# One task list with early positions of its own, and weight tiles loaded one by one into the freed tiles of high and low halves

## Chip, cores and metric

The kernel runs on one core of one Trainium2 chip. The metric is the device time of one execution in microseconds (us); the median of the runs is quoted, and a profile of one execution stands behind all rows.

## What is computed

Attention over 8 batches of 8 heads (576 positions, head size 64) with rotary embedding, followed by a soft mixture of experts over all 4608 tokens:

```python
q_rot, k_rot = rotate(q), rotate(k)
attn = softmax(q_rot @ k_rot.T / sqrt(64)); x = (attn @ v) as [4608, 512]
logits = x @ phi                              # 8 experts x 4 slots
slot_input = softmax(logits, tokens).T @ x
slot_out[e] = relu(slot_input[e] @ w1[e]) @ w2[e]     # w1: 8x512x1024, w2: 8x1024x512
out = softmax(logits, slots) @ slot_out
```

## The kernel before

The 64 heads are worked as 32 **pairs**. For each pair p the kernel runs the same set of named tasks:

- `load0`, `load1` (line 144, SyncE's queue SP): q and k of the pair into the tile `x_in`, of which there are two; so the load of pair p+2 waits until pair p has left `x_in`.
- `spin0`, `spin1` (L149, GpSimd, here POOL): products with cosine and sine, four instructions each; `join` (L153, VectorE, here DVE): their sum.
- `high0`, `high1` (L158, ScalarE, here ACT): casts of q and k to 16 bits, written into a tile `hl`; `low` (L162, DVE): what the casts lost, into the same `hl`, after which `x_in` is free.
- nine m units (`m00` to `m31`, `m_rem`): four matmuls on TensorE (PE, L182 or L190) of high halves into one of three score tiles `s_ps` in PSUM, and a DVE reduction (L184 or L192) that reads it; then `m_min` (DVE, L196), `m_turn` (PE, L203), `m_half` (ACT, L207) and `m_rows` (two DMAs on SP, L212 and L213), which put the row maxima into the tile `peak`.
- nine t units (`t0` to `t8`): sixteen matmuls (L229), the last four with `peak`, into an `s_ps`, and an exponential on ACT (L230) into `a_t`.
- nine `av` units (L245, PE): times v into `o_ps`; then `o_out` (ACT, L253), sums (`add1`, `add2` on DVE, `total` on PE, L273, `total_out` on ACT, L278), and the division by way of DRAM (`send`, `spread`, `widen` on SP, `norm` on POOL).

The engines take their instructions in the order in which the program issues them. That order comes from the table `WHEN`: a position for every task, in beats of which one pair has four. In the main loop `beat` sorts the tasks by their position within a beat, and pair p's round issues each task for the pair that is due. Ahead of the loop stands code written out by hand: 23 dummy matmuls on PE (`heat(N_WARM)`, L634), the m units of pair 0 mixed with parts of pair 1, then 16 dummy matmuls (`heat(16)`), then `join`, `high0` and four m units of pair 1, and then all tasks whose position is negative.

The mixture needs 64 weight tiles of 512 KB. `load_w` loads them in the order of the list `order`: 24 during the pairs, 7 into the space that `x_in` leaves (`release_io`, by `trickle`). When the last pair is through with its t units, `release_stk` gives up the pool of the four `hl` tiles and loads four more there: one tile `wk`, then three. `release_att` then loads the constant `seg` and nine tiles (pool `wl`); the rest follow as the first 24 tiles are used. Behind the pairs, PE works through `ffn1` (L782), `ffn2_steps` (L806) and `combine` (L834), which runs twice over nine blocks of the output: the first time mixed with `ffn2_steps`, the second time after the last of them. Each combine block is copied to SBUF and sent out by a DMA of 512 KB.

Of the kernel before, what the change touches and what calls it, by code (L numbers as in the profile page):

```python
# [29 lines left out]
N_XT = 3  # L30
N_WA = 5
N_WB = 2
N_WE = 3
N_WL = 9
N_X = 4
N_CS = 1
# [31 lines left out]
def attn_softmoe(ctx, tc, qk, v, phi, w1, w2, cs, ident, sel, seg, out):  # L68
# [10 lines left out]
    trans = ctx.enter_context(ExitStack())  # L79
    vp = trans.enter_context(tc.tile_pool(name="vp", bufs=2))  # L80
    att = trans.enter_context(tc.tile_pool(name="att", bufs=1))
    early = ctx.enter_context(ExitStack())
    stk = early.enter_context(tc.tile_pool(name="stk", bufs=4))
    right = ctx.enter_context(ExitStack())
    io = right.enter_context(tc.tile_pool(name="io", bufs=1, side="right"))
    dram = ctx.enter_context(tc.tile_pool(name="dram", bufs=3, space=bass.MemoryType.DRAM))
# [392 lines left out]
    order[N_W:N_W] = swap[:-1]
    order.insert(N_W + N_CST + N_WA, swap[-1])  # L480

    def load_w(pool, bufs, tag="w_exp"):
        n = order[len(w_tiles)]
# [12 lines left out]

    def release_io():
        right.close()
        wa = ctx.enter_context(tc.tile_pool(name="wa", bufs=N_CST, side="right", reuse_waits="tile"))
        wx = ctx.enter_context(tc.tile_pool(name="wx", bufs=N_WA, side="right", reuse_waits="tile"))  # L500
        extra.extend((wx, wa))
        later.extend([(wa, N_CST)] * N_CST + [(wx, N_WA)] * N_WA)

    def trickle(p):
        if later:
            load_w(*later.pop(0))

    def release_stk():
        early.close()
        hx = ctx.enter_context(tc.tile_pool(name="hx", bufs=1, side="right", reuse_waits="tile"))  # L510
        extra.append(hx)
        load_w(hx, 1, "wk")
        we = ctx.enter_context(tc.tile_pool(name="we", bufs=N_WE, side="right", reuse_waits="tile"))
        for _ in range(N_WE):
            load_w(we, N_WE)

    def release_att():
        trans.close()
# [37 lines left out]
    def one(task):  # L556
# [56 lines left out]
    beat = sorted((when % 4, int(when // 4), name) for name, when in WHEN.items())  # L613

    load(0)
    for t, cc in ((1, 0), (1, 1), (0, 0), (0, 1)):
# [15 lines left out]
    def heat(n):  # L632
        for i in range(n):
            nc.tensor.matmul(o[:, 0, 0:HC], lhsT=lift, rhs=halves[0][:, KH, 0:HC], start=True, stop=True)  # L634

    heat(N_WARM)
    low(0)
    done.update((n, 0) for n in ("spin0", "spin1", "join", "high0", "high1", "low", "load0", "load1"))
    do("load0", 2)
    do("load1", 2)  # L640
    nc.sync.dma_start(out=phi_sb, in_=phi.rearrange("(c p) n -> p c n", p=P))
    nc.sync.dma_start(out=sel_sb, in_=sel)
    do("spin1", 1)
    do("spin0", 1)
    for j in range(4):
        for n in range(2):
            do(f"m{j}{n}", 0)
        if j == 2:
            join(1, 1)
            do("high1", 1)  # L650
    do("m_rem", 0)
    do("m_min", 0)
    do("m_turn", 0)
    do("m_half", 0)
    m_rows(0, nc.scalar)
    done.add(("m_rows", 0))
    heat(16)
    join(1, 0)
    done.add(("join", 1))
    do("high0", 1)  # L660
    for j in range(2):
        for n in range(2):
            do(f"m{j}{n}", 1)
    do("low", 1)
    do("load0", 3)
    do("load1", 3)
    do("spin0", 2)
    do("spin1", 2)
    for when, name in sorted((when, name) for name, when in WHEN.items()):
        for p in range(NPAIR):  # L670
            if when + 4 * p < 0:
                do(name, p)

    for p in range(NPAIR):
        for _, back, name in beat:
            do(name, p - back)
        if not extra and ("low", NPAIR - 1) in done:
            release_io()

    p = NPAIR - 1  # L680
# [1 line left out]
        trickle(p)  # L682
    while pending:
        step(p)
    release_stk()
    for name in ("add1", "add2", "av4", "av5", "av6", "total", "total_out", "av7", "av8", "o_out"):
        do(name, p)
    steady.close()
# [252 lines left out]
```

## Time and profile before

| | us |
|---|---|
| median of 3 runs (lowest, highest) | 581.12 (580.03, 581.63) |
| the profiled execution: its time | 580.32 |
| the profiled execution: its span | 578.5 |
| busy in the span: PE, DVE, ACT, POOL | 527.7, 426.9, 330.7, 286.6 |

The profiled execution takes 1.8 us more than its span, and is 0.8 us below the median. The stages follow each other in the span: about 12 us until the first m unit, then a start in which the pairs get into step, then 30 pairs in a steady rhythm, then from about 500 us the mixture. A row of a timeline gives start, duration, engine, line and instruction; "x6" merges six of a kind, and brackets hold the idle time before and who ended it. SPq rows are the issue of a DMA, not its transfer. A row of windows gives one stretch: length, busy time of each engine with its count, TensorE's granted clock (1.00 is 2.4 GHz, 0.50 is 1.2 GHz), the share of the DMA engines and GB/s.

### The profile page before, as it was taken

To read this page: it belongs to the slowest core of one execution; us is meant where nothing else is said; L and a number is where in the kernel's file an instruction comes from. 1 tells how busy PE (TensorE), PEld (TensorE's weight loads), DVE (VectorE), ACT (ScalarE), POOL (GpSimd) and SP (SyncE) were. 2 spreads that over 40 slices of the span, in tenths; PEclk is the share of its full clock that TensorE was granted. 3 is DMA by queue.
4 is the path that set the end of the run, shared out by engine and by line. 5 is a ranking of instruction groups with operands and counts; after the bars stand their busy time and mean duration, and the time that the engine had idled before them with its cause. 6 is when DMAs were issued, how large, how long until landed. Compare 5 with 4: busy or idle time off the path is not lost.

```text
span 578.5 us, 23626 instructions
## 1 busy us (share of the span) xinstructions
PE 527.7 (91%) x10310; PEld 353.2 (61%) x10310; DVE 426.9 (74%) x643; ACT 330.7 (57%) x640; POOL 286.6 (50%) x332
## 2 busy tenths in 40 slices
PE   4669999999999998999999999999999999889991
PEld 2347667667766676666676767676766665634551
DVE  5788788889887897888889988988888752342261
ACT  2146557566657665766566666666666666315651
POOL 2865575576666685655655766566657010011100
PEclk9679999999999999999999999999999999989996
DMA  7244555555555555655655556555634245699999
GB/s 253 85 164 128 184 183 184 184 184 184 184 183 183 184 185 180 187 183 147 202 177 170 186 178 202 171 175 184 191 127 130 66 137 156 206 350 349 349 366 301
DMA packets 71735, 111.65 MB, mean 193 GB/s; under 512 B 20176, under 2 KB 47568, under 8 KB 71632
## 3 DMA queue, kind: packets, MB, share of 16 engines
q1 hardware_dynamic: 71618, 110.15, 59.0%
q8 instruction: 81, 1.33, 0.9%
q14 instruction: 22, 0.18, 0.1%
q10 hardware_dynamic: 14, 0.00, 0.0%
HBM read 99.93 MB, written 9.58 MB: 189 GB/s over the span
## 4 chain that ended last, share of the span: by engine, by line
PE 63%; DVE 12%; DMA 11%; ACT 6%; SPq 3%; issue 3%; POOL 0%; DVEq 0%; ACTq 0%
PE o_ps L245 17%; PE s_ps L229 17%; PE s_ps L273 7%; PE s_ps L182 5%; DMA rc<-s 4%; DVE nm L184 4%; DMA x_in<-in_qk 3%; SPq L284 3%; DVE hl L162 3%; PE s_ps L347 2%; PE s_ps L782 2%; DMA r_row<-rr 2%; PE s_ps L365 2%; ACT xn L356 1%; DVE x_in L153 1%
## 5 line engine op out<-in xcount | busy, mean ns | idle before, releaser
L149 POOL TENSOR_TENSOR x_in<-x_in,cs_sb 128x288 f32<-128x288 f32 x248 | 214.9, 899 | 130.8 <-DMA x_in<-in_qk 115.9
L184 DVE TENSOR_REDUCE nm<-s_ps 128x2 f32<-128x576 f32 x256 | 182.7, 751 | 55.7 <-PE s_ps L182 55.5
L230 ACT ACTIVATE a_t<-s_ps 128x576 f32<-128x576 f32 x256 | 160.8, 651 | 84.5 <-PE s_ps L229 72.8
L229 PE MATMUL s_ps<-hl 64*64 64x288 f16 x3456 | 160.1, 286 | 7.3 <-ACT xn L356 5.0
L245 PE MATMUL o_ps<-a_t,v_in 64*64 64x288 f32 x2048 | 163.6, 407 | 0.7 <-ACT xt L253 0.3
L229 PEld LDWEIGHTS <-hl 64*64 64x64 f16 x3456 | 102.0, 107 | 43.5 <-issue 28.8
L182 PE MATMUL s_ps<-hl 64*64 64x288 f16 x1024 | 84.5, 295 | 13.0 <-DVE nm L184 9.0
L229 PE MATMUL s_ps<-peak,lift 64*64 64x288 f16 x1152 | 91.9, 284 | 1.5 <-DMA peak<-mr 1.4
L307 POOL TENSOR_TENSOR xt<-xt,rb 128x576 f32<-128x576 f32 x30 | 48.8, 1626 | 71.3 <-DMA rb<-r_row 61.7
L245 PEld LDWEIGHTS o_ps<-a_t,v_in 64*64 64x64 f32 x2048 | 72.9, 133 | 17.1 <-ACT xt L253 4.5
L182 PEld LDWEIGHTS <-hl 64*64 64x64 f16 x1024 | 45.5, 106 | 36.7 <-issue 20.3
L158 ACT CAST hl<-x_in 128x576 f16<-128x576 f32 (+1 forms) x66 | 43.1, 655 | 24.4 <-DVE x_in L153 22.6
L153 DVE TENSOR_TENSOR x_in<-x_in 128x1152 f32<-128x1152 f32 (+2 forms) x36 | 54.6, 1517 | 2.7 <-POOL x_in L149 2.2
L278 ACT ACTIVATE s<-s_ps,bits 128x576 f32<-128x576 f32 x32 | 23.7, 742 | 48.3 <-PE s_ps L273 24.2
L260 DVE TENSOR_TENSOR c_t<-a_t 128x1152 f32<-128x1152 f32 x32 | 46.5, 1454 | 0.0
L162 DVE TENSOR_TENSOR hl<-x_in,hl 128x1152 f16<-128x1152 f32 x32 | 44.7, 1398 | 1.8 <-ACT hl L158 1.8
L229 PEld LDWEIGHTS <-lift 64*64 64x64 f16 x1152 | 40.3, 107 | 4.0 <-issue 2.6
L273 PE MATMUL s_ps<-a_t,pick 128*32 128x288 f32 x384 | 36.7, 406 | 0.0
L253 ACT COPY xt<-o_ps 128x576 f32<-128x576 f32 x32 | 20.5, 640 | 13.7 <-PE o_ps L245 13.7
L192 DVE TENSOR_REDUCE nm<-s_ps 128x2 f32<-128x576 f32 x32 | 24.1, 753 | 2.1 <-PE s_ps L190 0.9
L273 PEld LDWEIGHTS s_ps<-a_t,pick 128*32 128x32 f32 x384 | 16.4, 110 | 14.3
L263 DVE TENSOR_TENSOR c_t<-c_t,a_t 128x576 f32<-128x576 f32 x32 | 24.0, 750 | 0.1
(174 smaller groups left out, 536.4 us busy)
## 6 DMA issues: line engine op xcount, KB each, us to landing
x_in<-in_qk SPq DMA_DIRECT2D x62, 576.0 KB
w_exp<-in_w SPq DMA_DIRECT2D x63, 512.0 KB
v_in<-in_v SPq DMA_DIRECT2D x32, 576.0 KB
rb<-r_row SPq DMA_DIRECT2D x60, 144.0 KB
out<-w_exp SPq DMA_DIRECT2D x16, 512.0 KB
rc<-s SPq DMA_DIRECT2D x120, 4.5 KB
x_in<-in_qk SPq DMA_DIRECT2D x4, 288.0 KB
out<-w_exp SPq DMA_DIRECT2D x4, 256.0 KB
```

The lines of the kernel that those rows point to most:

```text
L149: eng.tensor_tensor(out=x[:, :, c], in0=x[:, :, c], in1=cs_sb[:, :, c], op=ALU.mult)
L153: nc.vector.tensor_tensor(out=x[:, t, 0, c], in0=x[:, t, 0, c], in1=x[:, t, 1, c], op=ALU.add)
L158: nc.scalar.copy(out=halves[p][:, 1 + t, c], in_=loaded[p][:, t, 0, c])
L162: nc.vector.tensor_tensor(out=hl[:, 0:4:3], in0=x[:, :, 0], in1=hl[:, 1:3], op=ALU.subtract)
L182: nc.tensor.matmul(s[rows[c], h, 0:HC], lhsT=hl[rows[h], QH, at:at + D], rhs=hl[rows[h], KH, half[n]], start=True, stop=True)
L184: nc.vector.tensor_reduce(out=nms[p][:, n, j:8:4], in_=s[:, :, 0:HC], axis=AX.X, op=ALU.max, negate=True)
L229: nc.tensor.matmul(s[rows[h ^ n], n, 0:HC], lhsT=lhs, rhs=rhs, start=(i == 0), stop=(i == 3))
L230: nc.scalar.activation(out=weights_of(p, b).rearrange("p (n x) -> p n x", n=2), in_=s[:, :, 0:HC], func=AF.Exp, scale=SCALE)
L245: nc.tensor.matmul(o[rows[h], n, 0:HC], lhsT=vt[r, b, n], rhs=a[r, half[n]], start=(b == 0), stop=(b == KB - 1))
L260: nc.vector.tensor_tensor(out=cts[p], in0=ats[p, 0], in1=ats[p, 1], op=ALU.add)
L273: nc.tensor.matmul(s[32 * i:32 * i + 32, n, 0:HC], lhsT=pick[:, n:n + NS], rhs=parts[cut][:, half[n]], start=first, stop=last, tile_positi ...
L307: eng.tensor_tensor(out=xts[p], in0=xts[p], in1=rbs.pop(p), op=ALU.mult)
```

## The change

**One list.** A second table, `EARLY`, gives the tasks of the first four pairs positions of their own, the dummy matmuls and constants among them. All tasks are put into one list, sorted and issued; the code by hand and `beat` are gone. From about pair 3 on, the order on every engine is that of before.

**Weight tiles in freed `hl` tiles.** The pool `stk` of the `hl` tiles is never given up. A new task `reuse` at beat 4.1 of pairs 28, 29 and 30 loads one weight tile into the `hl` tile of that pair, and after the last pair a fourth follows. `wk` becomes an `hl` tile; the pools that lie behind it move, and the load of `seg` has no tile to wait for any more.

```diff
+EARLY = {
+    "consts": (-31.889,), "heat0": (-31.727,), "spin1": (None, -30.178, -8.102, -2.333),
+    "low": (-29.941, -14.757, 0.917, 3.519), "load0": (None, None, -29.48, -13.395),
...
+    stk = ctx.enter_context(tc.tile_pool(name="stk", bufs=N_STK))
...
-    early = ctx.enter_context(ExitStack())
-    stk = early.enter_context(tc.tile_pool(name="stk", bufs=4))
...
-    def release_stk():
-        early.close()
-        hx = ctx.enter_context(tc.tile_pool(name="hx", bufs=1, side="right", reuse_waits="tile"))
-        extra.append(hx)
-        load_w(hx, 1, "wk")
-        we = ctx.enter_context(tc.tile_pool(name="we", bufs=N_WE, side="right", reuse_waits="tile"))
-        for _ in range(N_WE):
-            load_w(we, N_WE)
+    def reuse_stk(p):
+        if p >= NPAIR - N_STK:
+            load_w(stk, N_STK, "hl", swap[-1] if p == NPAIR - N_STK else None)
...
+        "reuse": lambda p: p < NPAIR - 1 and reuse_stk(p),
...
-    heat(N_WARM)
-    low(0)
...
-    heat(16)
-    join(1, 0)
-    done.add(("join", 1))
-    do("high0", 1)
...
-    for p in range(NPAIR):
-        for _, back, name in beat:
-            do(name, p - back)
+    seq = [(at, name, p) for name, ats in EARLY.items() for p, at in enumerate(ats) if at is not None]
+    early_set = {(name, p) for _, name, p in seq}
+    seq.extend((when + 4 * p, name, p) for name, when in WHEN.items() for p in range(NPAIR)
+               if (name, p) not in early_set and when + 4 * p < 4 * NPAIR)
+    seq.sort()
+    for i, (at, name, p) in enumerate(seq):
+        do(name, p)
...
-    release_stk()
+    reuse_stk(p)
```

**VectorE, from the last m units of pair 0 on.** `nm_194` and `nm_193` belong to pair 0, `nm_278` and `nm_265` to pair 1; `hl<-x_in,hl` is `low`, a `TENSOR_TENSOR` of 128x576 half a `join`, one of 128x2x576 a whole one. Before:

```order
L184 TENSOR_REDUCE nm_194<-s_ps 128x2 x2
L192 TENSOR_REDUCE nm_194<-s_ps 128x2
L196 TENSOR_REDUCE nm<-nm_194 128x9
L153 TENSOR_TENSOR x_in<-x_in 128x576
L184 TENSOR_REDUCE nm_278<-s_ps 128x2 x4
L162 TENSOR_TENSOR hl<-x_in,hl 128x2x576
L153 TENSOR_TENSOR x_in<-x_in 128x2x576
L162 TENSOR_TENSOR hl<-x_in,hl 128x2x576
```

Now:

```order
L202 TENSOR_REDUCE nm_193<-s_ps 128x2 x2
L210 TENSOR_REDUCE nm_193<-s_ps 128x2
L171 TENSOR_TENSOR x_in<-x_in 128x576
L202 TENSOR_REDUCE nm_193<-s_ps 128x2
L214 TENSOR_REDUCE nm<-nm_193 128x9
L180 TENSOR_TENSOR hl<-x_in,hl 128x2x576
L202 TENSOR_REDUCE nm_265<-s_ps 128x2 x4
L171 TENSOR_TENSOR x_in<-x_in 128x2x576
```

The second half of `join(1)` goes ahead of pair 0's last m unit and its `m_min`, `low(1)` ahead of pair 1's first four m units, and `low(2)` is gone from here: it now follows the `m_min` of pair 1. On PE the 16 dummy matmuls move behind those four m units.

**ScalarE, from the casts of pair 1 to the first exponentials.** Before:

```order
L158 CAST hl<-x_in 128x576
L207 ACTIVATE mr<-s_ps 9x128
L212 DMA peak_104<-mr 2x4x128
L213 DMA peak_104<-mr 2x1x64
L158 CAST hl<-x_in 128x576 x3
L230 ACTIVATE a_t<-s_ps 128x576 x6
```

Now:

```order
L176 CAST hl<-x_in 128x576 x2
L225 ACTIVATE mr<-s_ps 9x128
L230 DMA peak_104<-mr 2x4x128
L231 DMA peak_104<-mr 2x1x64
L176 CAST hl<-x_in 128x576
L248 ACTIVATE a_t<-s_ps 128x576
L176 CAST hl<-x_in 128x576
L248 ACTIVATE a_t<-s_ps 128x576 x6
```

Both casts of pair 1 now precede the DMAs that send pair 0's maxima, and the first exponential goes between the casts of pair 2.

**SyncE, the last weight loads of the pairs.** Before:

```order
L304 DMA rb<-r_row 64x576 x2
L493 DMA w_exp<-in_w 128x2x512 x3
L493 DMA wk<-in_w 128x2x512
L493 DMA w_exp<-in_w 128x4x256 x3
L525 DMA seg_in<-in_seg 128x320
L493 DMA w_exp<-in_w 128x4x256 x9
```

Now:

```order
L322 DMA rb<-r_row 64x576 x2
L509 DMA hl<-in_w 128x2x512
L509 DMA w_exp<-in_w 128x2x512
L509 DMA w_exp<-in_w 128x4x256 x2
L509 DMA hl<-in_w 128x4x256
L509 DMA w_exp<-in_w 128x4x256 x9
```

Two more `hl` loads stand further ahead, behind the `rb` loads of pairs 27 and 28, and `seg_in` has moved to the start of the program; so four tiles of the group that followed the last pair have become one.

## Rows read from the trace of the kernel before

**Rows 1.** Windows: three stretches of the start, one of the steady part.

```profile
10.00:20.00 10.00, 5.60 (x47) 2.35 (x45) 9.36 (x14) 1.54 (x3) 7.33 (x9) 0.75 0.67 240
20.00:30.00 10.00, 6.79 (x69) 3.84 (x69) 6.34 (x9) 0.94 (x2) 6.21 (x8) 0.74 0.01 2
30.00:40.00 10.00, 6.81 (x104) 5.53 (x105) 7.11 (x10) 3.93 (x7) 6.70 (x9) 0.66 0.66 236
...
102.00:117.00 15.00, 14.05 (x301) 9.98 (x300) 12.30 (x19) 9.27 (x17) 8.49 (x9) 1.00 0.55 176
```

**Rows 2.** Timeline of PE: first matmuls of `total` of pair 1 and of pair 31.

```profile
64.05 0.69 PE L273 MATMUL s_ps<-c_t,pick 128*32 128x288 f32 x8
...
500.16 0.69 PE L273 MATMUL s_ps<-c_t,pick 128*32 128x288 f32 x8
```

**Rows 3.** Timeline of DVE, from the first m unit to `join(3)`.

```profile
13.20 4.08 DVE L184 TENSOR_REDUCE nm<-s_ps 128x2 f32<-128x576 f32 x6
...
20.53 0.17 DVE L196 TENSOR_REDUCE nm<-nm 128x9 f32<-128x18 f32 x1
20.62 1.18 DVE L153 TENSOR_TENSOR x_in<-x_in 128x576 f32<-128x576 f32 x1
...
25.42 2.75 DVE L184 TENSOR_REDUCE nm<-s_ps 128x2 f32<-128x576 f32 x4 [3.62 <-PE s_ps L182]
...
32.02 1.36 DVE L162 TENSOR_TENSOR hl<-x_in,hl 128x1152 f16<-128x1152 f32 x1 [1.31 <-ACT hl L158]
...
40.00 0.17 DVE L196 TENSOR_REDUCE nm<-nm 128x9 f32<-128x18 f32 x1
...
40.11 1.97 DVE L153 TENSOR_TENSOR x_in<-x_in 128x1152 f32<-128x1152 f32 x1
```

**Rows 4.** Timeline of the other engines in the same stretch.

```profile
20.98 4.04 PE L634 MATMUL s_ps<-hl,lift 128*128 128x288 f16 x16
...
30.74 1.25 ACT L158 CAST hl<-x_in 128x576 f16<-128x576 f32 x2 [6.84 <-DVE x_in L153]
...
31.89 1.18 ACT L230 ACTIVATE a_t<-s_ps 128x576 f32<-128x576 f32 x2
...
32.59 0.99 PE L182 MATMUL s_ps<-hl 64*64 64x288 f16 x8 [3.67 <-ACT a_t L230]
...
33.30 6.80 POOL L149 TENSOR_TENSOR x_in<-x_in,cs_sb 128x288 f32<-128x288 f32 x9 [7.10 <-DMA x_in<-in_qk]
...
43.70 0.55 SPq L213 DMA_DIRECT2D peak<-mr  x1
...
45.72 0.56 PE L229 MATMUL s_ps<-hl 64*64 64x288 f16 x12
```

**Rows 5.** Windows: three stretches between changes of TensorE's clock.

```profile
15.00:25.00 10.00, 6.70 (x41) 3.11 (x44) 6.66 (x10) 1.61 (x3) 10.00 (x13) 0.50 0.32 115
26.00:32.00 6.00, 1.98 (x40) 1.19 (x40) 4.71 (x6) 1.26 (x3) 0.21 (x1) 1.00 0.24 73
32.00:38.50 6.50, 5.31 (x70) 4.05 (x71) 5.19 (x7) 2.27 (x4) 5.20 (x7) 0.50 0.80 298
```

**Rows 6.** Windows: three stretches of the mixture.

```profile
545.60:560.60 15.00, 14.29 (x156) 8.54 (x148) 8.54 (x14) 7.97 (x16) 0.00 (x0) 1.00 1.09 371
560.60:578.50 17.90, 5.42 (x30) 3.99 (x28) 5.35 (x8) 4.25 (x8) 0.00 (x0) 0.70 0.94 305
...
503.01:545.61 42.60, 38.86 (x411) 18.55 (x415) 11.34 (x32) 17.04 (x42) 6.16 (x12) 0.96 1.09 348
```

**Rows 7.** Timeline: exponential of `t8(28)`, then SP's queue up to the last outputs.

```profile
452.29 0.65 ACT L230 ACTIVATE a_rem<-s_ps 128x576 f32<-128x576 f32 x1
...
456.61 0.53 SPq L168 DMA_DIRECT2D v_in<-in_v  x1
...
499.18 2.25 SPq L493 DMA_DIRECT2D w_exp<-in_w  x3
...
560.61 10.34 SPq L838 DMA_DIRECT2D out<-w_exp  x8
```

More of the change, by code (lines that the diff above doesn't have):

```diff
@@ L32 @@
 N_WB = 2
-N_WE = 3
+N_STK = 4
 N_WL = 9
@@ L43 @@
 N_WARM = 23
+N_HEAT = 16
 N_CST = 2
@@ L59 @@
     "natural_out": 11.0916,
+}
+EARLY = {
[5 rows of a table added]
+    "m11": (-20.653, -13.607, -1.237, 6.307), "m_rem": (-20.46, -2.313, 4.26), "join_q": (None, -18.844),
+    "m30": (-17.958, -0.95, 3.636), "m_min": (-17.434, 0.445, 4.981), "m_turn": (-17.397, 0.922, 5.439),
+    "high0": (None, -17.087, -2.029, 1.011), "load1": (None, None, -16.982, -10.183),
+    "high1": (None, -16.326, -1.679, 0.953), "m_half": (-14.891, 0.96, 5.519), "rows_first": (-9.645,),
[5 rows of a table added]
+    "add2": (3.694, 7.44), "av8": (4.168, 8.276), "o_out": (4.21, 8.288), "total": (5.45,), "total_out": (5.566,),
+    "send": (6.413,),
 }
@@ L478, in attn_softmoe, with load_w @@
     order = [n for n in range(8 * E) if n not in swap]
[L479 to L483, printed above, removed]
+    def load_w(pool, bufs, tag="w_exp", n=None):
+        n = order.pop(0) if n is None else n
         layer, rest = divmod(n, 4 * E)
@@ L501, in release_io @@
         extra.extend((wx, wa))
-        later.extend([(wa, N_CST)] * N_CST + [(wx, N_WA)] * N_WA)
+        later.extend([(wa, N_CST, "w_exp", n) for n in swap[:-1]] + [(wx, N_WA)] * N_WA)
     def trickle(p):
@@ L611, in do @@
             plan[name](p)
-    beat = sorted((when % 4, int(when // 4), name) for name, when in WHEN.items())
     load(0)
@@ L634, in heat @@
             nc.tensor.matmul(o[:, 0, 0:HC], lhsT=lift, rhs=halves[0][:, KH, 0:HC], start=True, stop=True)
-    heat(N_WARM)
-    low(0)
[L638 to L656, printed above, removed]
-    heat(16)
-    join(1, 0)
-    done.add(("join", 1))
-    do("high0", 1)
[L661 to L669, printed above, removed]
-        for p in range(NPAIR):
-            if when + 4 * p < 0:
-                do(name, p)
@@ L674, in attn_softmoe, with join_part, rows_first, load_consts @@
-    for p in range(NPAIR):
-        for _, back, name in beat:
-            do(name, p - back)
-        if not extra and ("low", NPAIR - 1) in done:
+    def join_part(t):
+        return lambda p: join(p, t)
+    def rows_first(p):
+        m_rows(p, nc.scalar)
+    def load_consts(p):
+        nc.sync.dma_start(out=phi_sb, in_=phi.rearrange("(c p) n -> p c n", p=P))
+        nc.sync.dma_start(out=sel_sb, in_=sel)
+    plan.update({"heat0": lambda p: heat(N_WARM), "heat1": lambda p: heat(N_HEAT), "consts": load_consts,
+                 "join_k": join_part(1), "join_q": join_part(0), "rows_first": rows_first})
@@ new lines, in attn_softmoe @@
+    done.update((n, 0) for n in ("spin0", "spin1", "join", "high0", "high1", "load0", "load1", "load_v", "m_rows"))
+    done.update((n, 1) for n in ("load0", "load1", "join"))
+    seq = [(at, name, p) for name, ats in EARLY.items() for p, at in enumerate(ats) if at is not None]
+    early_set = {(name, p) for _, name, p in seq}
+    seq.extend((when + 4 * p, name, p) for name, when in WHEN.items() for p in range(NPAIR)
+               if (name, p) not in early_set and when + 4 * p < 4 * NPAIR)
@@ L678, in attn_softmoe @@
+    seq.sort()
+    for i, (at, name, p) in enumerate(seq):
+        do(name, p)
+        if not extra and ("low", NPAIR - 1) in done and (i + 1 == len(seq) or seq[i + 1][0] // 4 > at // 4):
             release_io()
@@ L790, in ffn1_turn @@
         if f == 0:
-            hts[grp] = (extra[2].tile([P, 2, 4, P], F32, name="wk") if grp else wp.tile([P, 2, 4, P], F32, name="w_exp", bufs=N_W))
+            hts[grp] = (stk.tile([P, 2, 4, P], F32, name="hl") if grp else wp.tile([P, 2, 4, P], F32, name="w_exp", bufs=N_W))
         t = ps_t.tile([P, 512], F32, name="t_ps")
@@ L820, in gather @@
                                  start=(grp + a == 0), stop=(grp + a == 2))
-        sl = (extra[2].tile([P, 256], F32R, name="kl") if mh else tail.tile([P, 256], F32R, name="sl"))
+        sl = (tail.tile([P, 256], F32R, name="kl") if mh else tail.tile([P, 256], F32R, name="sl"))
         nc.scalar.copy(out=sl, in_=rp[:, 0:256])
```

10 rows, old and new, of tables (EARLY, WHEN) are left out of this document.

## Prediction, made before the changed kernel ran

> **What bounds the kernel now.** I read the windows first, to find the stages with slack. In the steady part PE is busy 14.05 of 15.00 us at a granted clock of 1.00, while in the three stretches from 10 to 40 us it is busy 5.60, 6.79 and 6.81 of 10 at 0.75, 0.74 and 0.66 [rows 1]. So the pairs are bound by PE, and the start is not. The pace of the steady part comes from the first matmuls of `total`: from pair 1 to pair 31 it takes 500.16 - 64.05 = 436.1 us, 14.54 per pair [rows 2]. The order on every engine is unchanged there, so what the start gains arrives at the end as it is, unless the rhythm changes (third rival).
>
> Next I read the start on DVE, whose queue links everything: a pair's maxima must be through `m_min` before its t units may end. After 16 dummy matmuls of 4.04 us on PE [rows 4], DVE waits 3.62 us for the first m unit of pair 1; later it waits 1.31 us for casts, and the `m_min` of pair 1 ends at 40.00 + 0.17 = 40.17 [rows 3]. A second chain is to be seen on the other engines: POOL waits 7.10 us for `x_in` of pair 3, because that tile is held until `low(1)`; and PE waits 3.67 us for an exponential that stands behind two casts in ACT's queue (30.74 and 31.89) [rows 4].
>
> Last the mixture: there the DMA engines move 348 GB/s at a share of 1.09 from 503 us on, 371 while the first half of the outputs is made, 305 in the last 17.9 us [rows 6]. That looks like a bound by DMA, and the second part of the change takes bytes away from it; the third part below says why I think little of it.
>
> **The change, part by part.**
>
> *Start, up to `m_min(0)`.* The same reductions as before, but the second half of `join(1)` (1.18 us) now stands ahead of `m_min(0)`: it ends near 20.7 + 1.2 = 21.9 instead of 20.70 [rows 3]. Both casts of pair 1 follow `join` directly and need 1.25 us for two [rows 4], so they end near 22.3.
>
> *`low(1)` moves ahead of the m units of pair 1.* It takes some 1.35 us (`low(2)`: 1.36 [rows 3]), from 22.3 to 23.7; before, `low(1)` was behind four reductions that end at 28.17 [rows 3]. `x_in` is free some 5.8 us earlier (before at 29.4, 1.35 later than 28.1), and POOL's wait of 7.10 us falls to 1 or 2; the spins of pair 3 are then ready before DVE asks for them. There is a price: `low(1)` used to run while POOL was idle, and now POOL is at work on pair 2. The nearest row is `join(3)`: beside POOL's spins it took 1.97 us against 1.36 for an operation of the same length in the clear [rows 3]. GPSIMD Engine Reference of the Trainium skill, section Key points, says the same as a rule: GpSimd shares its SBUF interfaces with VectorE and contends with operations that have two SBUF inputs. By that rule this change gains 0.6 us less here; the trace agrees with the size. In return `join(3)` now falls into a time without spins. I take +0.3 us for the pair of effects, between 0 and +0.6.
>
> *Four reductions of pair 1, then the dummies.* 2.75 us as before [rows 3]: to about 26.4. The fourth unit is issued on PE some 1.2 us before that, and the 16 dummies follow, to about 25.2 + 4.0 = 29.2 [rows 4]. `join(2)` hides under them. They used to cover PE's wait for `join(1)`; now they stand in front of real work, and DVE stays idle for about 2 us until the next m unit. So of the old wait of 3.62 us only 1.6 are gained here; the rest comes from `low` and `join(2)`, which no longer follow.
>
> *Eight reductions to `m_min(1)`.* At 0.67 us each (six in 4.08 [rows 3]) DVE needs 5.4; before, seven took from 33.30 (end of `low(2)`) to 40.0, 6.7 us, in between t units and half of it at the lower clock [rows 3, 5]. I take 6.3: from 29.7 to 36.0, and `m_min(1)` ends at 36.2 instead of 40.17, that is -4.0. The wait of 3.67 us is gone, since the first exponential no longer stands behind two casts.
>
> *`low(2)` and `join(3)`, to `t0(1)`.* Both now follow `m_min(1)`: 1.36 + 1.36 to 38.9; before, `join(3)` alone, at 42.08. That is -3.2. From there to the landing of `peak` nothing changes: a cast, `m_half`, two DMAs. But before, `t0(1)` started at 45.72, about 0.5 us after `peak` can have landed (issues end at 44.25 [rows 4]; I estimate 1.0 more), because PE was still busy with pair 0, and only its last matmuls need `peak`: 0.5 to 0.9 us of slack, of which the new order can use 0.6. So `t0(1)` moves by -3.2 - 0.6 = **-3.8**, with +0.3 from POOL **-3.5 us**. From `t0(1)` on PE was busy all the time, and the rest moves with it.
>
> *Bounds of this term.* The biggest unknown is the clock. Before, it was 0.50 from 15 to 25 us, 1.00 after the dummies, 0.50 again from 32 after a stretch in which PE was busy 1.98 of 6.00 us [rows 5]. I assume that the dummies bring it back at about 29.5 and that no wait of 3.67 us drops it again. Upper end of the gain: the clock is back when they begin, they take 2.0 instead of 4.0, and the term is -5.5. Lower end: it stays at 0.50 until `m_min(1)`; PE's work there (five t units of 0.49, two `av` of 0.49, eight m units of 0.12, 4.4 us in all, by start-to-start times behind 45.72) would be 8.8 in a stretch of 6.5, which costs 2.3: -1.2.
>
> *`seg` and its copy on POOL.* Its load goes to a time when DMA is idle (0.01 in [rows 1]); the copy, some 0.5 us, falls into POOL's wait for pair 3. Nothing; if that wait were gone, 0.5 us of POOL, which is not the bound.
>
> *Weight tiles behind the last pairs.* The `hl` load of pair 28 gets its turn on SP just ahead of the `v_in` load at 456.61, and its tile was read last by `t8(28)`, whose exponential starts at 452.29 [rows 7]: SP doesn't wait, and 4 us of pairs out of step would be needed before it did. Queued behind it are `v_in`, `send` and `m_rows`; the next `send` is 5 us later, so the 1.5 us of transfer (512 KB at 348 GB/s [rows 6]) delays nobody. Pairs 29 and 30 are alike. After 499.18, when three tiles and `seg` used to follow [rows 7], one `hl` tile is left; one `wl` tile needs no wait any more, the other eight still wait for the last `av`. So 2 x 0.524 + 0.164 = 1.2 MB less is left for the mixture, at 348 GB/s 3.5 us.
>
> How much of that arrives? The second half of the outputs is 9 x 0.524 = 4.72 MB, which PE releases from 560.6 on, whatever came before. In the last 17.9 us 305 x 17.9 = 5.46 MB moved [rows 6], so only 0.74 MB were left over at 560.6, and the two last outputs of the first half, 0.52 MB, would be under way then in any case. 0.22 MB at 371 GB/s is 0.6 us; I take **-0.4**, between 0 and -2.0 (all of the 0.74). The rest of the 3.5 us ends in idle DMA between 545 and 560, where PE sets the pace.
>
> *Sum.* Against the profiled execution: 580.32 - 3.5 - 0.4 = 576.4. That execution is 0.8 under the median, so the median should become 581.12 - 3.9 = **577.2 us**.
>
> **Rivals.**
>
> 1. *The mixture is bound by DMA to the end.* For it: a share over 1 from 503 us on. Against it: the 0.74 MB above. Then the tail gives -2.0: 581.1 - 3.5 - 2.0 = 575.6; with the early clock 573.6.
> 2. *The clock stays low, or drops again.* The dummies come later and PE's work around them is thin. At 1.2 to 2.3 us less, 578.4 to 579.5. For it: [rows 5] show a drop in just such a place. Against it: the wait that preceded the drop is gone.
> 3. *The start's gain is lost in the pairs.* The pairs' pace is not PE alone: if SP's, POOL's or DMA's steps meet the pairs otherwise, the old distance returns within some pairs, and only the tail stays: about 580.7.
> 4. *Slower.* The same mechanism, further: two queues settle in a longer rhythm, say SP holds `m_rows` behind a load that waits for `low`. The steady part has 30 periods, so 0.13 us per period on 14.54 [rows 2] eat up the 3.9, and 0.2 give +2.1: 583.2. Against it: the order from pair 4 on is the same.
>
> **How the numbers follow.** No change means within 0.3%, 1.7 us, about what a measurement can tell here: 579.4 to 582.9. The forecast, with early and late clocks near it (575.1 to 578.3), has 0.50; rival 1 0.11, rival 2 0.17 (all faster but a little at its end), rival 3 0.13, rival 4 0.09. So faster 0.77, same 0.14, slower 0.09. The range takes in rival 1 with the early clock, rival 2 and the better part of rival 3: 573.6 to 580.6; left out are rival 4 and half of rival 3.
>
> **What would show it.** `low(1)` near 22 us and POOL's wait before pair 3 under 2.5; dummies ending near 29 and the granted clock 1.00 soon after; `m_min(1)` near 36, `t0(1)` near 42; the `total` of pairs 1 and 31 both 3 to 4 us earlier. In the mixture, three `hl` loads before 490 and a gap in DMA's share near 503 or 550 to 560. Wrong would be: a `total` of pair 31 that moves less than that of pair 1 (rivals 3, 4), or a distance from there to the end that shrinks by more than 1 us (rival 1).

## The result, and the profile after

| us | before | changed |
|---|---|---|
| median, 20 runs each | 580.21 (577.19 to 585.57) | 574.29 (571.08 to 578.24) |
| profiled execution: time, span | 580.32, 578.5 | 578.09, 576.3 |
| first matmul of `total`: pair 1, pair 31 | 64.05, 500.16 | 60.59, 495.28 |
| from `total` of pair 31 to the end of the span | 78.34 | 81.02 |

The ratio is 0.9896, 95% interval 0.9869 to 0.9923: faster by 5.9 us (the difference of the medians; 4.5 to 7.6 by the interval) where 3.9 were forecast. Of the 2.9 us between the forecast time of 577.2 and 574.29, 0.9 are the old kernel's own median, 581.12 in three runs and 580.21 in twenty. The profiled execution of the changed kernel is one of the longest of its 20, and its -2.2 us understates the change; why, the last two rows of the table and the windows below show.

VectorE's timeline of the changed kernel, answering to [rows 3] (L180 is `low`, L171 `join`, L202 and L210 reductions of m units, L214 `m_min`):

```profile
22.51 1.36 DVE L180 TENSOR_TENSOR hl<-x_in,hl 128x1152 f16<-128x1152 f32 x1 [0.43 <-ACT hl L176]
23.78 2.75 DVE L202 TENSOR_REDUCE nm<-s_ps 128x2 f32<-128x576 f32 x4
27.54 1.57 DVE L171 TENSOR_TENSOR x_in<-x_in 128x1152 f32<-128x1152 f32 x1 [1.01 <-POOL x_in L167]
30.03 0.76 DVE L202 TENSOR_REDUCE nm<-s_ps 128x2 f32<-128x576 f32 x1 [0.91 <-PE s_ps L200]
...
36.23 0.17 DVE L214 TENSOR_REDUCE nm<-nm 128x9 f32<-128x18 f32 x1
36.32 1.35 DVE L180 TENSOR_TENSOR hl<-x_in,hl 128x1152 f16<-128x1152 f32 x1
37.58 1.35 DVE L171 TENSOR_TENSOR x_in<-x_in 128x1152 f32<-128x1152 f32 x1
```

`low(1)` is at 22.51, `m_min(1)` ends at 36.40 (before 40.17) and `join(3)` at 38.93 (before 42.08). The other engines, answering to [rows 2, 4]: the dummies, GpSimd's spins of pair 3, `t0(1)`, and the `total` of pairs 1 and 31:

```profile
25.64 4.02 PE L644 MATMUL s_ps<-hl,lift 128*128 128x288 f16 x16
27.87 7.16 POOL L167 TENSOR_TENSOR x_in<-x_in,cs_sb 128x288 f32<-128x288 f32 x8
42.03 0.54 PE L247 MATMUL s_ps<-hl 64*64 64x288 f16 x12
60.59 0.69 PE L291 MATMUL s_ps<-c_t,pick 128*32 128x288 f32 x8
495.28 0.69 PE L291 MATMUL s_ps<-c_t,pick 128*32 128x288 f32 x8
```

GpSimd no longer waits for pair 3, `t0(1)` is 3.7 us earlier, `total(1)` 3.5. Windows of the changed kernel, answering to [rows 5, 6] (the columns are those of rows 1):

```profile
15.00:28.60 13.60, 7.45 (x54) 3.45 (x50) 12.01 (x16) 1.51 (x3) 13.60 (x16) 0.54 0.49 183
28.60:29.70 1.10, 1.10 (x9) 0.46 (x9) 0.52 (x1) 0.55 (x1) 1.10 (x1) 0.50 0.93 367
29.80:38.50 8.70, 7.75 (x176) 5.48 (x170) 7.88 (x11) 4.93 (x9) 5.23 (x7) 1.00 0.04 16
...
495.28:503.10 7.82, 6.17 (x91) 3.76 (x87) 2.22 (x9) 2.54 (x6) 0.86 (x1) 1.00 0.88 285
503.10:513.40 10.30, 9.59 (x57) 4.33 (x61) 4.09 (x14) 1.39 (x8) 1.39 (x5) 0.55 1.07 345
...
556.23:576.30 20.07, 6.66 (x36) 5.03 (x36) 6.04 (x9) 5.18 (x9) 0.00 (x0) 0.74 0.89 278
```

The start has one stretch at half clock where before had two. It ends between 29.7 and 29.8. But between the last pair and the mixture the clock was at half for some 10 us, from 504.2 to 514.5. The last row begins with the second `combine` (L824, first matmul that reads the tile `kl`; below, `kl` stands for the start of that matmul): the DMA engines are busy for 0.89 of it and move 278 GB/s. The kernel before has a stretch of 3.4 us at half clock behind the last pair, and moves 310 GB/s from its second `combine` on:

```profile
513.30:516.70 3.40, 3.28 (x16) 0.78 (x20) 0.07 (x1) 0.00 (x0) 0.00 (x0) 0.50 1.09 347
...
559.08:578.50 19.42, 6.69 (x36) 5.06 (x36) 6.04 (x9) 5.18 (x9) 0.00 (x0) 0.73 0.94 310
```

### The profile page after: what moved, and what is told of

Its sections match the earlier page's. It is cut to its first block, busy times and chain, and to the rows that moved or that the text cites. A ratio compares the mean times of both kernels' runs of the same rounds, so it can differ in the third digit from the quotient of the medians.

```text
span 576.3 us, 23629 instructions
## 1 busy us (share of the span) xinstructions
PE 528.5 (92%) x10310; PEld 352.5 (61%) x10310; DVE 431.7 (75%) x643; ACT 330.2 (57%) x640; POOL 286.3 (50%) x332
## 3 DMA queue, kind: packets, MB, share of 16 engines
q1 hardware_dynamic: 71618, 110.15, 58.9%
## 4 chain that ended last, share of the span: by engine, by line
PE 62%; DMA 11%; DVE 10%; ACT 6%; SPq 4%; issue 3%; POOL 2%; DVEq 0%; ACTq 0%; POOLq 0%
PE o_ps L263 16%; PE s_ps L247 16%; PE s_ps L291 7%; PE s_ps L200 5%; DMA x_in<-in_qk 4%; DMA rc<-s 4%; DVE nm L202 3%; SPq L302 3%; DVE hl L180 3%; PE s_ps L365 2%; PE s_ps L772 2%; POOL x_in L167 2%; ACT a_t L248 2%; PE s_ps L383 2%; ACT xn L374 1%
## 5 line engine op out<-in xcount | busy, mean ns | idle before, releaser
L202 DVE TENSOR_REDUCE nm<-s_ps 128x2 f32<-128x576 f32 x256 | 182.9, 751 | 51.9 <-PE s_ps L200 51.1
L263 PE MATMUL o_ps<-a_t,v_in 64*64 64x288 f32 x2048 | 161.9, 405 | 0.7 <-ACT xt L271 0.3
L247 PEld LDWEIGHTS <-hl 64*64 64x64 f16 x3456 | 101.1, 106 | 42.1 <-issue 27.3
L247 PE MATMUL s_ps<-peak,lift 64*64 64x288 f16 x1152 | 90.4, 283 | 1.3 <-DMA peak<-mr 1.3
L200 PEld LDWEIGHTS <-hl 64*64 64x64 f16 x1024 | 44.6, 106 | 35.7 <-issue 21.2
L171 DVE TENSOR_TENSOR x_in<-x_in 128x1152 f32<-128x1152 f32 (+2 forms) x36 | 54.5, 1513 | 2.3 <-POOL x_in L167 1.8
L296 ACT ACTIVATE s<-s_ps,bits 128x576 f32<-128x576 f32 x32 | 23.7, 741 | 48.3 <-PE s_ps L291 28.3
L278 DVE TENSOR_TENSOR c_t<-a_t 128x1152 f32<-128x1152 f32 x32 | 49.6, 1551 | 0.0
L180 DVE TENSOR_TENSOR hl<-x_in,hl 128x1152 f16<-128x1152 f32 x32 | 46.0, 1438 | 0.9 <-ACT hl L176 0.9
L210 DVE TENSOR_REDUCE nm<-s_ps 128x2 f32<-128x576 f32 x32 | 24.0, 751 | 1.4 <-PE s_ps L208 0.2
```

What stands on the lines that cost most here:

```text
L171: nc.vector.tensor_tensor(out=x[:, t, 0, c], in0=x[:, t, 0, c], in1=x[:, t, 1, c], op=ALU.add)
L180: nc.vector.tensor_tensor(out=hl[:, 0:4:3], in0=x[:, :, 0], in1=hl[:, 1:3], op=ALU.subtract)
L200: nc.tensor.matmul(s[rows[c], h, 0:HC], lhsT=hl[rows[h], QH, at:at + D], rhs=hl[rows[h], KH, half[n]], start=True, stop=True)
L202: nc.vector.tensor_reduce(out=nms[p][:, n, j:8:4], in_=s[:, :, 0:HC], axis=AX.X, op=ALU.max, negate=True)
L247: nc.tensor.matmul(s[rows[h ^ n], n, 0:HC], lhsT=lhs, rhs=rhs, start=(i == 0), stop=(i == 3))
L263: nc.tensor.matmul(o[rows[h], n, 0:HC], lhsT=vt[r, b, n], rhs=a[r, half[n]], start=(b == 0), stop=(b == KB - 1))
```

## The experiments

In this part a difference in us is the ratio times the kernel before's median on the same chip.

**The two halves of the change, and both again.** e1 is the changed kernel with the pools of before:

```diff
-    stk = ctx.enter_context(tc.tile_pool(name="stk", bufs=N_STK))
+    early = ctx.enter_context(ExitStack())
+    stk = early.enter_context(tc.tile_pool(name="stk", bufs=4))
...
-    reuse_stk(p)
+    release_stk()
```

> The changed kernel's list with the early positions, but weight tiles and seg loaded as before (all of them behind the last pair). The first theory is the prediction's sum: the start is worth -3.5 us and comes through the pairs unchanged, so total(1) near 60.6 instead of 64.05, total(31) near 496.7 instead of 500.16, time about 576.7 against 580.2 of before (ratio 0.994). The second theory: the start also changes the rhythm of the pairs, as the first profile of the change seems to show (total(31) 4.9 us earlier, total(1) only 3.5): then total(31) near 495.3 and a time about 575.3 (ratio 0.9916). The third theory puts the surplus of the measured -5.9 into the tail: then this kernel stays at -3.5.

e2 has the start by hand and the `beat` of before, and the new use of the `hl` tiles:

```diff
-    for i, (at, name, p) in enumerate(seq):
-        do(name, p)
+    heat(N_WARM)
+    low(0)
...
+        for _, back, name in beat:
+            do(name, p - back)
```

> The start and the pairs' order of before, but weight tiles taken into the freed tiles of high and low halves behind pairs 28 to 31, and seg loaded early. The prediction's sum gives -0.4 us (ratio 0.9993), total(31) unchanged at about 500. The third theory (the mixture is bound by DMA to its end, the rival of the prediction) gives -2.0 to -2.5 us (ratio 0.996). If the early weight tiles got in the way of the last pairs, total(31) would be late by up to 1 us and the time +0.5.

e3 is the changed kernel as it is.

> The changed kernel once more, beside its two halves on one chip. If the two halves add up, its difference from before is the sum of the two runs above within 1 us: by the prediction -3.9, by the second theory -5.3, by the third -5.5 to -6. If TensorE's clock in the mixture decides, its single times spread over some 7 us again (571 to 578), the long ones with the lower mean clock.

| | ratio to before | us | `total(1)`, `total(31)` |
|---|---|---|---|
| e1, start alone | 0.9930 (0.9903 to 0.9957) | -4.1 | 60.66, 497.38 |
| e2, weight tiles alone | 0.9975 (0.9945 to 1.0006) | -1.5 | 63.16, 499.50 |
| e3, both | 0.9917 (0.9885 to 0.9948) | -4.8 | 60.20, 493.11 |

The halves add up within their intervals. The start is worth what was forecast within its interval; the weight tiles are worth more than 0.4, though by time alone e2 can't be told from no change. The second theory is neither shown nor excluded: from `total(1)` to `total(31)` the new start took 434.69 us in the first trace, 436.72 in e1 and 432.91 in e3, against 436.11 and 436.34 with the old one. Over all twelve traces of the new order, those below among them, it is 432.9 to 438.4, with a mean of 435.0; ten of them lie below both old ones. The 1.4 us that the first profile seemed to gain in the pairs lie inside that scatter, but a gain of about 1 us on average would fit as well, and two traces of the old start are too few to tell.

Where the mixture differs is seen behind `total(31)`. Two windows of e1, 20 us up to the second `combine` and from there to the end:

```profile
534.79:554.79 20.00, 19.32 (x218) 10.98 (x211) 8.97 (x15) 10.52 (x23) 0.86 (x1) 1.00 1.09 362
554.79:575.80 21.01, 7.36 (x36) 5.46 (x36) 6.13 (x9) 5.17 (x9) 0.00 (x0) 0.68 0.95 317
```

In e1's trace the clock stayed at 1.00 from the last pair up to the second `combine`, and the second `combine` came 57.4 us after `total(31)`, 1.5 us sooner than in the trace of before (58.9). The end came at 78.42 all the same, where before had 78.34: 317 GB/s for 21.01 us are 6.66 MB, 1.94 MB over the 4.72 of the second half.

**Dummies for the clock behind the last pair.** e4 puts 16 dummy matmuls into the waits there, e8 only those 13 that delay nothing:

```diff
+    def hum(t, n):
+        for _ in range(n):
+            nc.tensor.matmul(t[:, 1, 128:128 + HC], lhsT=lift, rhs=peaks[0][:, 0:HC], start=True, stop=True)
...
         sg[p] = t = bank2()
+        if p == NPAIR - 1:
+            hum(t, 4)
...
+        if ps[0] == NPAIR - 1:
+            hum(t, 6)
...
+    hum(sp, 3)
     prev = (0, 0, ffn1(0, 0))
```

> The changed kernel with 16 dummy matmuls of 128x288 put into the waits of TensorE between the last total and the first ffn1 (4, 6, 2, 1 and 3 of them; about 0.12 us each at full clock), where the profile of the change shows a granted clock of 0.50 for 10.2 us. If the drop of the clock there follows from TensorE's thin work and is what makes the runs differ, the stretch at 0.50 becomes shorter or vanishes and the median falls by 1 to 2 us below the changed kernel's, with less spread. If the clock goes its own way, the dummies only cost: between 0 and +1.5 us.

> The changed kernel with 13 dummy matmuls in TensorE's waits between the last total and the first ffn1 (4 in front of sums_wide, 6 in front of the last logits, 3 in front of ffn1), without the three that made e4's chain 0.8 us longer. If they keep the clock at 1.00 there, the first matmul of the last combine (kl) starts 57.3 to 57.7 us after total(31), the span ends 19.6 to 20.2 us behind that, and no run shows a mean clock under 0.975; the median is 1 to 1.5 us below the changed kernel's. If the drop comes all the same, kl starts at 58.5 to 61 and nothing is gained.

e4: 0.9894 (0.9864 to 0.9924), 575.23 us against e3's 575.68 on the same chip. e8: 0.9896 (0.9855 to 0.9937). In both traces the clock stays at 1.00. The 27 runs of the changed kernel's orders with such dummies (e4, e8 and e11, e12 below) have mean clocks of 0.975 and up; of 30 runs without (the first 20 and e3) nine are at 0.973 or less and take 576.3 to 578.2 us, the other 21 take 571.1 to 576.6. So the drop is real and costs these runs some microseconds, and with the new loads the dummies take it away. With the old loads no such effect is seen: two of the 12 runs of e9 below are at 0.972 or less, as two of the 12 of e1 are without dummies. The lower median that both expectations named did not come, since the pairs scatter as much. In e4 three extra dummies stood in front of a transpose and waited with their tile for a VectorE copy: 0.8 us on the chain to `ffn1`.

e9 is e1 with the same 13 dummies, e10 is e8 with a part of the weights left out:

```diff
-        nc.sync.dma_start(out=wt, in_=src)
-        w_tiles[n] = wt
+        if n < 8 * E - 8:
+            nc.sync.dma_start(out=wt, in_=src)
+        w_tiles[n] = wt if n < 8 * E - 8 else w_tiles[n - 8]
```

> The same 13 dummies on the kernel with the new start alone (weights and seg loaded as before). It puts a price on the tail part of the change with TensorE's clock out of the way. By the prediction's step (the outputs are released by TensorE, whatever came before) the tail part is worth 0.4 us: this kernel's span ends 19.6 to 20.6 us after kl like the other's, and it is 0.4 us slower. If two bounds stand side by side and the later one wins, the DMA engines hold the end at 78.4 us after total(31) however early kl comes: 20.8 to 21.1 us after kl, DMA share at 1.0 or more up to the end, and 1 to 1.5 us slower than the one above.

> The kernel with both parts and 13 dummies, with its last eight weight tiles (4.2 MB) left out: the second output half's second group uses the first group's weights, so the output is another one. If the changed kernel's mixture is bound by TensorE and the outputs alone, kl starts at the same 57.3 us after total(31) and the span ends at the same 19.6 to 20.2 us behind it. If bytes left over still hold its end, that distance falls to 18 us or so, and if weights make TensorE wait before, kl comes earlier as well.

The 20 us up to the second `combine`, and from there to the end, in e8:

```profile
532.01:552.01 20.00, 19.32 (x231) 11.14 (x219) 8.97 (x15) 11.05 (x24) 0.86 (x1) 1.00 1.09 364
552.01:572.40 20.39, 6.70 (x36) 5.06 (x36) 6.04 (x9) 5.17 (x9) 0.00 (x0) 0.73 0.88 281
```

and in e10:

```profile
531.67:551.67 20.00, 19.32 (x230) 11.15 (x219) 8.97 (x15) 11.05 (x24) 0.86 (x1) 1.00 0.59 196
551.67:571.70 20.03, 6.63 (x36) 5.06 (x36) 6.04 (x9) 5.17 (x9) 0.00 (x0) 0.77 0.89 278
```

e10 settles what bounds the changed mixture where the clock holds: with 4.2 MB less the DMA share ahead is 0.59 instead of 1.09, and nothing else moves. `kl` comes 56.84 us after `total(31)` in both, the end 20.03 after it instead of 20.39; the two runs of e10 have a median of 574.25 us, those of e8 574.48. TensorE and the outputs themselves set the end, and further early loads would gain nothing here. e9 was 575.76 us against e8's 574.48 on the same chip (0.9926, 0.9901 to 0.9952, against 0.9896): 1.3 us, as the two bounds have it, but the intervals overlap, and the clock fell in its profiled execution in spite of the dummies (`kl` at 60.76, end at 80.94), so its trace shows only that case.

By traces, microseconds after `total(31)`:

| clock behind the last pair | old loads: `kl`, end | new loads: `kl`, end |
|---|---|---|
| 1.00 throughout | e1: 57.41, 78.42 | e2: 57.28, 76.90; e4: 57.66, 77.86; e6: 56.82, 77.22; e8: 56.84, 77.23; e11: 56.83, 76.36; e12: 56.83, 76.28 |
| 3.4 us at half | before: 58.92, 78.34 | e3: 58.53, 78.79; e5: 58.14, 77.90 |
| longer at half | e9 (6.8 us): 60.76, 80.94 | first trace (10.2 us): 60.95, 81.02; e7 (10.2 us): 61.24, 81.04 |

(e5 to e7, e11 and e12 follow below.) With the new loads the end comes 19.4 to 20.4 after `kl`. With the old ones it comes 19.4 and 20.2 after it where the clock fell, but 21.0 in e1: there the DMA engines hold it at 78.4, and the earlier `kl` is lost. So the weight tiles are worth 0.6 to 2.1 us where the clock holds, 1.4 against the mean of the six, 77.0, and nothing that the traces can tell where it falls. On the side of the old loads this rests on one trace, e1. Three pairs of timings on one chip each point the same way, before and e2 by 1.5 us, e1 and e3 by 1.7, e9 and e8 by 1.3; none of them is clear of noise by itself.

The early load of `seg` does not bring `ffn1` forward: in e1 its copy on GpSimd runs only at 504.88, and still the first matmul of `ffn1` starts 12.83 us after `total(31)`, against 12.80 to 12.81 in e6, e8, e11 and e12.

**Single pieces of the start.** e5 leaves out the second dummies (`N_HEAT = 0`), e6 and e7 put one `low` back:

```diff
-    "low": (-29.941, -14.757, 0.917, 3.519), "load0": (None, None, -29.48, -13.395),
+    "low": (-29.941, -9.7, 0.917, 3.519), "load0": (None, None, -29.48, -9.69),
```

```diff
-    "low": (-29.941, -14.757, 0.917, 3.519),
+    "low": (-29.941, -14.757, -5.0, 3.519),
```

(e6 moves `load1` of pair 3 to -9.68 as well, e7 the casts of pair 2 to -5.03 and -5.02.)

> The changed kernel without its second group of dummy matmuls (0 instead of 16, which took 4.02 us from 25.64 on). What they are for: the prediction's step says they bring the clock back and cost about 2 us of waiting on VectorE. The changed kernel's trace has VectorE waiting 1.01 us for GpSimd and then only 0.91 us for TensorE there. If they only cost, the first m unit's reduction behind them starts at 29.1 instead of 30.03, m_min(1) ends near 35.5 instead of 36.4 and total(1) starts near 59.7 instead of 60.59. If they carry the clock, the granted clock stays at 0.50 for some microseconds longer, m_min(1) ends at 37.5 to 38.5 and total(1) starts at 61.5 to 63.

> The changed kernel with low(1) moved back behind the first four m units of pair 1, and the load of pair 3 behind it; the rest of the start as in the change. If the early low(1) matters through GpSimd (x_in free 5 us earlier, the prediction's wait of 7.10 us that falls to none), then the spins of pair 3 start 3 us later (near 31 instead of 27.87), join(3) has to wait for them and total(1) goes from 60.59 to 61.5 or later. If the gain of the start lies in what VectorE's queue holds ahead of m_min(1) (low(2) and the dummies), nothing is lost, since low(1) fits under the dummies: total(1) 59.8 to 60.8.

> The changed kernel with low(2) and the two casts it reads put back ahead of pair 1's second group of m units, as before the change. If VectorE's queue ahead of m_min(1) carries the start's gain, this gives back the 1.35 us of low(2) and up to 1.2 us of waiting for the casts: m_min(1) ends at 37.7 to 39 instead of 36.4. What of it reaches the pairs: join(3) follows m_min(1) directly then, so total(1) moves by 0 (if the end of join(3) decides) up to +2.5 (if m_min(1) decides). If the place of low(2) doesn't matter, both stay where they are.

*e5*, windows behind the place of the dummies, and VectorE's first m unit there:

```profile
28.60:33.10 4.50, 3.14 (x48) 2.64 (x51) 3.20 (x5) 2.43 (x4) 4.50 (x6) 0.50 0.32 126
33.20:38.00 4.80, 4.04 (x104) 2.97 (x100) 4.56 (x8) 2.51 (x5) 1.94 (x3) 1.00 0.02 3
```

```profile
29.16 0.74 DVE L202 TENSOR_REDUCE nm<-s_ps 128x2 f32<-128x576 f32 x1
```

In this execution both theories are right and cancel: VectorE starts 0.87 us earlier, the clock is back at 33.2 instead of 29.8, 3.4 us later, and `total(1)` is at 60.75 (60.59). Eight traces of the same start with 16 dummies (the first, e1, e3, e4, e8, e9, e10, e12) have `total(1)` at 60.10 to 61.29, so the trace shows no gain from the dummies. The timing is 0.9947 (0.9905 to 0.9988), and it leaves the question open: the execution in the trace is the fastest of e5's eight runs, and five of the others have mean clocks of 0.961 to 0.967, under all 30 runs of the changed kernel, and take 580.0 to 581.3 us. No trace shows where these lost their clock.

*e6*, `low(1)`, spins of pair 3, `join(3)`, `t0(1)`, and a window behind it:

```profile
25.43 1.86 DVE L180 TENSOR_TENSOR hl<-x_in,hl 128x1152 f16<-128x1152 f32 x1
```

```profile
31.47 7.17 POOL L167 TENSOR_TENSOR x_in<-x_in,cs_sb 128x288 f32<-128x288 f32 x8 [3.88 <-DMA x_in<-in_qk]
```

```profile
38.67 1.36 DVE L171 TENSOR_TENSOR x_in<-x_in 128x1152 f32<-128x1152 f32 x1 [2.19 <-POOL x_in L167]
```

```profile
40.96 0.78 PE L247 MATMUL s_ps<-hl 64*64 64x288 f16 x12 [2.19 <-ACT mr L225]
```

```profile
41.00:44.50 3.50, 3.50 (x40) 2.46 (x43) 2.23 (x3) 1.66 (x3) 3.50 (x3) 0.52 0.35 105
```

`m_min(1)` starts 1.36 us earlier than in the change, at 34.87, and still `total(1)` is at 62.81, 2.2 us later: GpSimd's spins come 3.6 us later, `join(3)` waits 2.19 us for them, the cast of its result and with it `m_half` of pair 1 on ScalarE wait for `join(3)`, TensorE waits 2.19 us for `m_half`, and the clock falls once more. 62.81 lies clear of the 60.10 to 61.29 of the eight traces. The timing, 0.9966 (0.9923 to 1.001), can't be told from those of e5 and e7.

*e7*, `low(2)` in its old place, `m_min(1)` and `join(3)`:

```profile
30.43 1.36 DVE L180 TENSOR_TENSOR hl<-x_in,hl 128x1152 f16<-128x1152 f32 x1 [1.31 <-ACT hl L176]
...
37.15 0.17 DVE L214 TENSOR_REDUCE nm<-nm 128x9 f32<-128x18 f32 x1
37.26 1.66 DVE L171 TENSOR_TENSOR x_in<-x_in 128x1152 f32<-128x1152 f32 x1
```

`low(2)` waits 1.31 us for its casts, as before the change. `m_min(1)` ends 0.9 us later, `join(3)` at 38.92 as in the change, and `total(1)` is at 61.04. That is 0.45 us after the first trace's and inside the 60.10 to 61.29 of the eight: the place of `low(2)` is worth little, and the trace can't say whether it is worth anything. 0.9945 (0.9903 to 0.9987).

**Eight dummies, and the loads in one lump.** e11 is e8 with `N_HEAT = 8`. e12 is e8 with the four `hl` loads together behind the last pair:

```diff
-        "reuse": lambda p: p < NPAIR - 1 and reuse_stk(p),
+        "reuse": lambda p: None,
...
-    reuse_stk(p)
+    for q in range(NPAIR - N_STK, NPAIR):
+        reuse_stk(q)
```

> Both parts, 13 dummies in the tail, and 8 instead of 16 dummies in the start. Without any, VectorE won 0.87 us behind them and lost it again to 4.4 us more at half clock, total(1) at 60.75. With 8 the clock could come back at the same time as with 16 (28.6) and VectorE's 0.9 us stays: total(1) near 59.8, time 0.8 us under the kernel above. If 8 don't bring it back in time, total(1) is at 60.5 to 60.8 as with 0 and 16, and the time is the same.

> Both parts and 13 dummies, but the four weight tiles for the freed hl tiles are requested together behind the last pair instead of one by one at beat 4.1 of pairs 28 to 30. Before the change the same loads waited for a pool that was given up as a whole (three of them until 499.18). If it is the tile-by-tile release that counts and not the early place on SyncE's queue, the first three go out as soon as the queue gets to them, near 484 to 487, kl starts 56.8 us after total(31), the span ends 19.5 to 20.4 us behind it and the time is that of the kernel with both parts and 13 dummies (574.5). If the early place counts, they go out at 495 or later, 1.05 MB more are left for the mixture, kl comes at 57.4 and the end at 78.4 us after total(31): 1.2 us slower.

e11: 573.35 us, 0.9869 (0.9839 to 0.9900), the lowest median of the study; `total(1)` at 59.66 against e8's 60.17, and below all eight traces with 16 dummies. The clock is back at 29.3, as with 16 (29.1 in e8), and VectorE's first reduction behind the dummies starts at 28.96, as the first theory had it. It beats the kernel before by 7.6 us, and e8 on the same chip by 1.1; its interval overlaps with e8's and the changed kernel's.

e12, the issue of the four `hl` loads:

```profile
485.07 9.23 SPq L517 DMA_DIRECT2D hl<-in_w  x4
```

The first three go out from 485.07 on and the fourth at 493.94, when pair 31 is through. In the change they went at 452.24, 465.45, 481.96 and 494.30; in before three waited until 499.18 [rows 7]. `kl` comes at 56.83, the end at 76.28 after `total(31)`, and the time is 573.92 us, 0.9848 (0.9806 to 0.9890). So the early place of the loads on the queue does not matter. What is left is that each waits for its own tile: with the whole pool given up, as in e1, the last three went out from 496.40 on, and `seg` and the nine `wl` tiles behind them.

## Why the prediction was right, and where not

- **Start, the times: right.** Forecast and measured: `low(1)` 22.3 and 22.51, dummies end 29.2 and 29.66, `m_min(1)` 36.2 and 36.40, `join(3)` end 38.9 and 38.93, `t0(1)` 42 and 42.03, `total(1)` 3 to 4 us earlier and 3.46. One trace against one flatters the forecast: the eight traces of the new start have 60.10 to 61.29, mean 60.6, the two of the old one 64.05 and 63.16 (e2), mean 63.6. So the start is worth 3.0 by the means, 1.9 to 4.0 from trace to trace. The 1.0 us that the working takes for the landing of `peak` stands in no row; `t0(1)` came when it was due all the same.
- **Start, the reason: half right.** The working put the gain on VectorE's queue ahead of `m_min(1)`, and named GpSimd's shorter wait beside it, priced at +0.3 together with the contention. e6 shows that the early `low(1)`, by way of GpSimd, is worth 2.2 of the 3.0. Without it `m_min(1)` may come as early as it likes; `join(3)` waits. The place of `low(2)` (e7, 0.45) and, in the one execution that was traced, the dummies (e5, 0.16) can't be told from the scatter of `total(1)`.
- **The +0.3 for contention** was not there on VectorE: `low(1)` took 1.36 beside the spins, as in the clear. GpSimd paid: the spin that started 0.05 us after it took 1.95 us, where its neighbours take 0.79.

```profile
22.56 1.95 POOL L167 TENSOR_TENSOR x_in<-x_in,cs_sb 128x288 f32<-128x288 f32 x1
```

In e6, where `low(1)` started 0.14 us after a spin, it took 1.86 itself. In both places the operation that started second was the longer one, and the time that GpSimd lost may be what `join(2)` waits for, 1.01 us, while the dummies run. The GPSIMD Engine Reference of the Trainium skill, section Key points, has GpSimd share its SBUF interfaces with VectorE; these rows agree with it.

- **Clock in the start: right.** 0.50 until 29.8 (assumed 29.5), and no second drop in the change. The latest return of the clock with 16 dummies, 31.0 in e9, has `total(1)` at 61.29, 0.7 after the first trace's; the 1.2 to 2.3 of rival 2 stood for a clock that stays low up to `m_min(1)`, which no trace shows. A second drop in the start came only in e6, behind the wait for `join(3)`.
- **Weight tiles, -0.4: mis-sized.** The step that failed is "which PE releases from 560.6 on, whatever came before". 560.6 belonged to an execution whose clock had fallen behind the last pair. In e1, where it held, `kl` comes 1.5 us sooner, 1.94 MB are left over then, and the DMA engines hold the end; the same sum for before's trace (310 GB/s in its last 19.42 us, 6.02 MB) leaves 1.30. So the term is 1.4 on average where the clock holds (0.6 to 2.1; its bounds were 0 to 2.0), and rival 1 was right for e1's kind of execution and wrong for the one profiled. Its sign, a distance from `total(31)` to the end more than 1 us shorter than before's 78.34, is seen in five of the six traces of the new loads at full clock. Three `hl` loads went out before 490, as forecast. Nor did the rest of the saved time end in idle DMA between 545 and 560: with the clock at 1.00 the share is 1.09 in the 20 us up to `kl` in e8 as in e1, and what the tiles took away is missing behind `kl`, where 1.01 MB are left over in e8 (281 GB/s for 20.39 us, less 4.72 MB). A share under 1 ahead of `kl` is to be seen in the first trace (0.83 from 540 to 545), whose `kl` came late.
- **Rivals 3 and 4** fell: what the start gained at `total(1)` was there at `total(31)` on average, 435.0 us later against 436.2. Single executions were up to 2.2 us longer than that (438.4 in e4).
- **The sum.** 3.0 for the start and 1.4 for the tiles where the clock holds, less on average, are 4.4 or less; the two timings give 5.9 (4.5 to 7.6) and 4.8 (3.0 to 6.7). What is over may lie in the pairs, which took 1.2 us less by the means above, or in the share of executions whose clock falls behind the last pair; no run settles it. The profiled -2.2 is explained by the end of its span: at the 77.0 of the traces with full clock instead of its 81.02 it would have taken 4.0 us less, 574.1, close to the median.

## What to carry to other kernels

Ask of a moved step not only what its own queue gains but which engine's input it frees: here one `low` ahead of four reductions released a tile to the load, the load to GpSimd, and GpSimd to the next `join`. A bound read from one execution holds for that execution's clock: before calling a transfer hidden, work out the sum for an earlier arrival of the engine that hides it. And when a pool's tiles become free one after the other, keep the pool and let each load wait for its own tile. Before a difference between two traces is given to an edit, look how far traces of one and the same code lie apart, and whether the profiled execution is a typical one of its runs.

## What was unexpected

- Behind the last pair TensorE was busy 6.17 of 7.82 us, in many short matmuls, and the clock still fell in some executions: not at all in e1, e2 and e6, for 3.4 us in before, e3 and e5, for 10.2 us in e7 and in the first trace of the change, which made that one 4 us longer.
- The clock also came back at different times in one and the same start with 16 dummies, and `total(1)` followed it: back at 28.3, 29.0 and 29.1 in e3, e4 and e8 with `total(1)` at 60.20, 60.10 and 60.17; at 29.8 to 29.9 in the first trace, e10 and e1 with 60.59, 60.71 and 60.66; at 30.6 in e12 with 60.88; at 31.0 in e9 with 61.29. Most of the scatter of `total(1)` goes with it.
- The pairs have an exact base rhythm with single late ones. In e4 the way from `total(12)` to `total(13)` took 19.51 us, against 15.6 to 16.1 in the first trace of the change, e1, e3, e5, e6 and e7 and 17.15 in before: GpSimd waited 4.9 us for a broadcast of `rb`, TensorE 2.53 for GpSimd (L391, `logits`), and the clock fell for 3.4 us:

```profile
227.66 0.66 PE L391 MATMUL s_ps<-xt,phi_sb 128*32 128x128 f32 x8 [2.53 <-POOL xt L325]
```

```profile
226.00:228.00 2.00, 0.34 (x8) 0.33 (x12) 0.00 (x0) 0.00 (x0) 1.79 (x2) 0.74 0.95 379
228.00:230.00 2.00, 2.00 (x40) 1.48 (x36) 1.03 (x3) 0.01 (x1) 2.00 (x4) 0.50 0.21 44
```

- From `kl` to the end took 19.45 us in e12 and 20.39 in e8, with `kl` 56.8 us after `total(31)` and the clock at 1.00 up to it in both. Why stays open.
